# Packing the quarter-wasted product of a two-layer expert kernel into half arrays, a block at a time, with the order of all engines made anew

## The chip, the cores and the metric

The kernel runs on one core of a Trainium2 chip. A core has five engines that run their own instruction streams in order: PE (matrix products; its weight loads, PEld, are separate instructions), DVE and ACT (elementwise work), POOL (here mainly the issuer of indirect DMAs) and SP (the issuer of plain DMAs). The metric is device time in microseconds for one execution; lower is better. Before the change the median of three runs is 1201.41 us (1190.59 to 1201.69).

## What is computed

```python
x  = attention_like_convolution(x, softmax(weight_gen))      # 14336 tokens x 192 channels, 7 taps
lg = x @ w_gate + log1p(exp(x @ w_noise)) * noise            # 8 experts
top2, top2_w = two largest of lg, softmax over the two
for e in range(8):                                           # each expert: 192 -> 1024 -> 192
    out[mask] += top2_w * (relu(x[mask] @ w1[e]) @ w2[e])
```

Inputs and outputs are fp32. The kernel carries each fp32 factor as a pair of fp16 numbers, a high part and a low part, and adds up the products of the parts.

## The kernel before, in words

**Front end.** Tokens come in 14 chunks of 1024. For a chunk, DVE does the convolution (13 multiplications and additions of 128x1536, lines 327 and 337), ACT and DVE split the result into high and low parts (lines 348, 352; tile `rec`, 384 fp16 values a token: 192 high parts, the low parts of channels 128 to 191, the low parts of channels 0 to 127), SP makes transposed copies (line 374), PE computes gate logits (line 381), and DVE picks the two experts and a row in each expert's queue (lines 449 to 558). POOL then scatters the 1024 tokens to the queues in HBM, `xg`, by 16 indirect DMAs (line 411), each behind a tiny memset (line 410). ACT squares the convolution's inputs ahead of it (line 273).

**Rounds and blocks.** Round c takes 256 rows from each of the 8 queues once chunk c is scattered: 8 blocks a round, 14 rounds, and a fifteenth with 128 rows a block. For a block, SP fetches the rows transposed (line 823) into `xT`, three tiles of 128 partitions: x0 the high parts of channels 0 to 127, x1 the high parts of channels 128 to 191 on the lower 64 partitions and their low parts on the upper 64, x2 the low parts of channels 0 to 127. Six `xT` buffers exist.

**First layer.** A block has four steps (two in the last round). A step (`mm1`, line 879) fills one PSUM bank `pm` with two of the eight 128-wide slices of the hidden layer: five products a slice, ten of 128x256 in all. One of the five is W_low x x1 (weight columns 384 to 511). Only the lower 64 of its 128 rows are needed; the upper 64 multiply a low part by a low part, which is negligible. ACT makes `hi` (line 894) and DVE `lo` (line 898) from the bank.

**Second layer.** `mm2` (line 919) takes `hi` and `lo` of a step as stationary operands: 12 products of 192 columns. At a block's end ACT scales the sums (line 931, tile `y`), and POOL adds them to the output by an indirect DMA for each 128 rows (line 936), two a block. In the last round each of these waits for the one before.

**Order.** Nothing is reordered on the chip. A planner (`Sched`) runs at build time: every piece of work is a generator that names its engine, a planned duration and what it waits for, and the planner lays the instructions down in the order in which they would start, ties within `WAIT` going to the higher number in `PR`. The generator `tensor` alternates the steps on PE: `mm1` of a step, then `mm2` of the step two before, so that ACT and DVE have time between. There are five slots, each with a `pm` bank and a `hi` and `lo` tile. The eight experts' weights are split once at the start; for experts in `LOWPE` the low parts are made on PE and ACT (lines 739 to 743), for the others on DVE (lines 710, 717, 719).

Of the kernel before, what the change touches and what calls it, by code (L numbers as in the profile page):

```python
# [8 lines left out]
F16 = mybir.dt.float16  # L9
# [6 lines left out]
P = 128  # L16
NTOK = 14336
NJ = NTOK // P
D = 192
# [22 lines left out]
NEAR = 2  # L42
HURRY = 12
# [6 lines left out]
LOWPE = (0, 4, 5, 6)  # L50
WAIT = 0.29
PR = dict(split=1.0, gate=8.7, conv1=12.1, conv=4.3, route=7.6, idle=8.7, scatter=1.8, stray=2.1, gates=5.7,
          finish=12.3, relu=11.4, norms=4.0, rows=9.0, wload=1.0, due=12.1, undue=4.3)
GL, AL, ML, UL, XL = 3.9, 0.9, 4.4, 17.1, 15.4
# [93 lines left out]
def moe_kernel(ctx, tc, x_lay, wgen, noise, wgn, w1, w2, xg, out):  # L148
# [630 lines left out]
    class Block:  # L779
        pass  # L780
# [16 lines left out]
    def prologues():  # L797

        for c, (k, b) in enumerate(ROUNDS):
# [31 lines left out]
            for e in range(E):  # L831
# [35 lines left out]
    def mm1(si):  # L867

        bi, s = steps[si]
        o = blist[bi]  # L870
        v = slot_of[si]
        pm = (psb if v < PM0 else late[0]).tile([P, 512], F32, name=f"pm{v}")
        for k in range(o.nf):
            f = s * o.nf + k
            w = wres[:, o.e * WE + f * FW:o.e * WE + (f + 1) * FW]
            dst = pm[:, k * o.b:(k + 1) * o.b]
            x0, x1, x2 = (o.xT[:, i, :o.b] for i in range(3))
            for i, (c0, m) in enumerate(((0, x0), (0, x2), (128, x1), (384, x1), (256, x0))):
                nc.tensor.matmul(dst, w[:, c0:c0 + 128], m, start=i == 0, stop=i == 4)  # L879
        hbuf[si] = pm  # L880
# [88 lines left out]
    def tensor():  # L969
# [12 lines left out]
        for si, (bi, s) in enumerate(steps):  # L982
# [10 lines left out]
            slot_of[si], prev_of[si], last[v] = v, last[v], si  # L993
            T["mm1", si] = yield ("PE", 1.09 * o.nf * o.b / 512, lambda: mm1(si), deps)
# [141 lines left out]
```

## Time and profile before

| | |
|---|---|
| median of 3 runs | 1201.41 us (1190.59 to 1201.69) |
| the profiled execution | 1206.64 us, its span 1204.7 us |
| PE busy | 1051.8 us (87%) |
| DVE busy | 825.7 us (69%) |
| POOL busy | 749.8 us (62%) |
| ACT busy | 526.0 us (44%) |
| mean granted PE clock | 0.950 of full speed |

The page sums each engine over the whole span. It also cuts the span into 40 slices of 30 us, with one digit for each (9 is busy 90% or more). A wait is shown behind a row as the idle time before it and what ended it. Since PE is pipelined, the recorded duration of one product is longer than the distance from its start to the next one's start; the distance is what a stream of products costs.

### The profile page before, as it was taken

The numbers are of one execution on the slowest core, as the hardware profiler recorded it, in microseconds if no ns is written. First come the engines' busy times: TensorE is split into PE (matmuls) and PEld (weight loads), VectorE is DVE, ScalarE is ACT, GpSimd is POOL, SyncE is SP. The second block draws the span as 40 slices with busy tenths as digits, with TensorE's granted clock in tenths as the row PEclk, the third lists the DMA queues.
The fourth block names the chain that finished last, engine by engine and source line by source line (L and its number), as shares of the span: only waits on it lengthen the run. The fifth ranks groups of instructions, "written<-read, shape, count | busy, mean of one in ns | idle before, by whom it ended". The sixth has DMA issues, their size and how long they took to land.

```text
span 1204.7 us, 27979 instructions
## 1 busy us (share of the span) xinstructions
PE 1051.8 (87%) x10862; PEld 953.8 (79%) x10862; DVE 825.7 (69%) x1552; ACT 526.0 (44%) x1191; POOL 749.8 (62%) x1013
## 2 busy tenths in 40 slices
PE   1414899797998999999999999989999889999995
PEld 0201499786997999889999889879898779999995
DVE  5898878686795969778887859678885343333331
ACT  6868573342443444443435344434343233333332
POOL 0004368477686868778684858778787867434333
PEclk9755999898998999999999999999999989999998
DMA  9993473665647577485748666365555545434341
GB/s 246 244 283 100 117 170 62 92 145 95 132 88 138 109 125 98 88 161 96 154 78 155 107 117 129 58 131 120 79 91 81 102 74 81 52 54 47 35 41 21
DMA packets 249686, 132.48 MB, mean 110 GB/s; under 512 B 182096, under 2 KB 242000, under 8 KB 247888
## 3 DMA queue, kind: packets, MB, share of 16 engines
q1 hardware_dynamic: 205392, 85.37, 32.3%
q0 software_dynamic: 44160, 45.31, 24.9%
q8 instruction: 85, 1.39, 0.5%
q14 instruction: 49, 0.40, 0.1%
HBM read 38.70 MB, written 58.10 MB: 80 GB/s over the span
## 4 chain that ended last, share of the span: by engine, by line
PE 52%; POOL 15%; DMA 10%; DVE 7%; issue 6%; ACT 6%; SPq 4%; another core or an unknown queue 0%; POOLq 0%; DVEq 0%; ACTq 0%
PE pm L879 27%; PE py L919 24%; POOL xg L411 8%; POOL out L936 7%; DMA xt<-x_lay 3%; DMA out<-y,token 3%; SPq L817 2%; DVE acc L337 2%; DVE tmp L327 2%; DVE lo L898 2%; DMA xg<-rec,pos 1%; DMA xT<-xg 1%; DMA wres<-w 1%; ACT junk L682 1%; ACT junk L273 1%
## 5 line engine op out<-in xcount | busy, mean ns | idle before, releaser
L879 PE MATMUL pm<-xT,wres 128*128 128x256 f16 (+1 forms) x4800 | 594.3, 271 | 30.2 <-DMA xT<-xg 23.4
L936 POOL DMA_INDIRECT out<-y,token x232 | 408.0, 1759 | 254.4 <-ACT y L931 89.3
L898 DVE SCALAR_TENSOR_TENSOR lo<-pm,hi 128x512 f16<-128x512 f32 x464 | 316.1, 686 | 301.1 <-ACT hi L894 261.4
L879 PEld LDWEIGHTS <-wres 128*128 128x128 f16 x4800 | 451.6, 99 | 83.4 <-DMA xT<-xg 21.9
L919 PE MATMUL py<-wres,hi 128*128 128x192 f16 x3712 | 503.3, 247 | 9.8 <-ACT hi L894 4.0
L894 ACT ACTIVATE hi<-pm 128x512 f16<-128x512 f32 x464 | 275.7, 596 | 507.4 <-PE pm L879 407.7
L919 PE MATMUL py<-wres,lo 128*128 128x192 f16 x1856 | 458.6, 247 | 4.5 <-issue 3.0
L919 PEld LDWEIGHTS <-hi 128*128 128x128 f16 x3712 | 341.6, 98 | 23.2 <-issue 8.9
L411 POOL DMA_INDIRECT xg<-rec,pos x224 | 292.0, 1304 | 76.4 <-issue 67.5
L919 PEld LDWEIGHTS <-lo 128*128 128x128 f16 x1856 | 182.3, 98 | 8.5 <-issue 5.5
L337 DVE TENSOR_TENSOR acc<-acc,tmp 128x1536 f32<-128x1536 f32 (+1 forms) x90 | 148.0, 1644 | 1.1
L327 DVE TENSOR_TENSOR tmp<-xt,wt 128x1536 f32<-128x1536 f32 (+1 forms) x90 | 148.2, 1646 | 0.7
L931 ACT ACTIVATE y<-py,gate 128x192 f32<-128x192 f32 x232 | 96.3, 417 | 78.0 <-PE py L919 37.6
L935 POOL MEMSET spacer<- 1x1 f32 x232 | 102.8, 443 | 0.1
L533 POOL TENSOR_SCALAR rec<-rr 128x8 f32<-128x8 f32 x14 | 3.2, 229 | 90.7 <-DVE rr L482 89.8
L410 POOL MEMSET spacer<- 1x1 f32 x224 | 53.3, 238 | 0.1
L273 ACT ACTIVATE junk<-xt 128x192 f16<-128x192 f32 x118 | 42.3, 359 | 23.9 <-DMA xt<-x_lay 22.0
L602 PE MATMUL sums<-ss,ones 128*128 128x2 f32 x32 | 8.1, 333 | 39.4 <-ACT junk L682 39.4
L602 PEld LDWEIGHTS sums<-ss,ones 128*128 128x128 f32 x32 | 7.1, 282 | 43.0 <-ACT junk L682 43.0
L739 PE MATMUL sums<-wres,dg 128*128 128x512 f32 (+1 forms) x48 | 29.3, 698 | 5.3 <-ACT wres L743 3.1
L352 DVE TENSOR_TENSOR rec<-acc,rec 128x512 f16<-128x512 f32 (+2 forms) x30 | 26.8, 900 | 3.1 <-ACT rec L348 2.7
L739 PEld LDWEIGHTS sums<-wres,dg 128*128 128x128 f32 x48 | 9.9, 230 | 22.3 <-ACT wres L743 10.4
(139 smaller groups left out, 514.8 us busy)
## 6 DMA issues: line engine op xcount, KB each, us to landing
xt<-x_lay SPq DMA_DIRECT2D x13, 1344.0 KB
out<-zrec SPq DMA_DIRECT2D x14, 768.0 KB
wres<-w SPq DMA_DIRECT2D x6, 768.0 KB
out<-y,token POOLq DMA_INDIRECT x232
xg<-rec,pos POOLq DMA_INDIRECT x224
wt<-wgen SPq DMA_DIRECT2D x14, 224.0 KB
wres<-w SPq DMA_DIRECT2D x6, 512.0 KB
wres<-w SPq DMA_DIRECT2D x12, 256.0 KB
```

The costliest lines, as they stand in the source:

```text
L273: nc.scalar.activation(q, xtile[s][:, i - first], AF.Square, accum_out=nrm[:, i:i + 1])
L327: V.tensor_mul(tm[key].rearrange("p j (h g) -> p j h g", h=H), xt[:, t:t + n].rearrange("p j (h g) -> p j h g", h=H), w[:, a:a + n].rearra ...
L337: ta = yield ("DVE", cc, lambda: V.tensor_add(tm["acc"], tm["acc"], tm["tmp"]), [])
L410: nc.gpsimd.memset(spacer, 0.0)
L411: i = nc.gpsimd.indirect_dma_start(out=xg, out_offset=bass.IndirectOffsetOnAxis(ap=idx, axis=0), in_=src, in_offset=None)
L879: nc.tensor.matmul(dst, w[:, c0:c0 + 128], m, start=i == 0, stop=i == 4)
L894: nc.scalar.activation(h[0][:, :n], pm[:, :n], AF.Relu)
L898: T["lo", si] = yield ("DVE", dve(n), lambda: nc.vector.scalar_tensor_tensor(h[1][:, :n], pm[:, :n], 0.0, h[0][:, :n], op0=OP.max, op1=OP. ...
L919: nc.tensor.matmul(dst, h[:, cols], w[:, c0:c0 + D], start=begin, stop=f == F // P - 1 and i == 2, skip_group_check=True)
L931: nc.scalar.activation(y[0], o.py[t // 2][:, (t % 2) * D:(t % 2 + 1) * D], AF.Copy, scale=gate_of[o.c][:, o.e, t:t + 1])
L935: nc.gpsimd.memset(spacer, 0.0)
L936: i = nc.gpsimd.indirect_dma_start(out=out, out_offset=bass.IndirectOffsetOnAxis(ap=token[o.c][:, o.e, t:t + 1], axis=0), in_=y[0], in_off ...
```

## The change

From the third round on (`PACK = 2`) the half-empty product is done in half arrays. A second transposed copy (`again`) puts channels 64 to 191 on the 128 partitions of a fourth tile in `xT`, so that the high parts of channels 128 to 191 lie on the upper 64 partitions too. `mm1` then does all steps of a block at once: four full products a slice, eight slices, and behind them eight products with 64 rows each, alternately on the lower and the upper half of the array, into two different PSUM banks. `tensor` lays a block's `mm1` down as one piece and lets one block's steps wait behind it (`BEHIND = 1`). The planner's numbers are other ones, and with them the order of everything; `LOWPE` has experts 4, 5, 7 in place of 0, 4, 5, 6.

```diff
-NEAR = 2
-HURRY = 12
+NEAR = 8
+HURRY = 9
...
+PACK = 2
+BEHIND = 1
+LOWPE = (4, 5, 7)
...
-                o.xT = (blk if v < 3 else late[1]).tile([P, 3, BMAX], F16, name=f"xT{v}", bufs=1)
-                note(nc.sync.dma_start_transpose(o.xT[:, :, :b], xg.bitcast(F16)[bass.ds(base[o.e], b), 0:RD]))
+                o.packed = c >= PACK
+                o.xT = (blk if v < 3 else late[1]).tile([P, 4, BMAX], F16, name=f"xT{v}", bufs=1)
+                note(nc.sync.dma_start_transpose(o.xT[:, 0:3, :b], xg.bitcast(F16)[bass.ds(base[o.e], b), 0:RD]))
+
+            def again(o):
+
+                note(nc.sync.dma_start_transpose(o.xT[:, 3:4, :b], xg.bitcast(F16)[bass.ds(base[o.e], b), 64:D]))
...
+                if c >= PACK:
+                    T["x", bi] = yield ("SP", 1.3, lambda: again(blist[bi]), [], 0.15 * nt)
...
-    def mm1(si):
+    def mm1(si, n):
...
+        for s in range(s0, s0 + n):
+            v = slot_of[si + s - s0]
+            pm = (psb if v < PM0 else late[0]).tile([P, 512], F32, name=f"pm{v}")
+            hbuf[si + s - s0] = pm
+            for k in range(o.nf):
+                f = s * o.nf + k
+                w = wres[:, o.e * WE + f * FW:o.e * WE + (f + 1) * FW]
+                dst = pm[:, k * o.b:(k + 1) * o.b]
+                parts.append((w, dst, k))
+                ops = [(0, x0), (0, x2), (128, x1), (256, x0)] + ([] if o.packed else [(384, x1)])
...
+        if o.packed:
+            m = len(parts) // 2
+            for a, b in zip(parts[:m], parts[m:]):
+                for (w, dst, k), h, x in ((a, slice(0, 64), x1), (b, slice(64, P), o.xT[:, 3, :o.b])):
+                    nc.tensor.matmul(dst, w[h, 384:512], x[h], start=False, stop=k == o.nf - 1, skip_group_check=True)
...
-            v = min(range(SLOTS if late else PM0), key=lambda i: last[i])
-            deps = [("x", bi), ("low1", o.e)] + ([("lo", last[v])] if last[v] >= 0 else [])
+            m = o.n if o.packed_(late) else 1
+            vs = sorted(range(SLOTS if late else PM0), key=lambda i: last[i])[:m]
+            deps = [("x", bi), ("low1", o.e)] + [("lo", last[v]) for v in vs if last[v] >= 0]
...
-                if len(pend) > DEPTH - 1 or r is None or r > sch.free["PE"] + 0.4:
+                if len(pend) > (DEPTH - 1 if m == 1 else o.n - 1 + BEHIND) or r is None or r > sch.free["PE"] + 0.4:
...
+            us = 1.09 * o.nf * o.b / 512 * m
+            if m > 1:
+                us = us * 0.9 + 0.2
+            t = yield ("PE", us, lambda: mm1(si, m), deps)
```

On PE in the middle of the run, before: the last product of a step's first layer (`pm`) and the second layer (`py`) of an earlier step (`hi1`, `lo1`). Numbers in names tell buffers and tiles apart.

```order
L879 MATMUL pm0_9249<-xT3_8731,wres_94 128x256
L919 LDWEIGHTS hi1_9203
L919 MATMUL py_9189<-wres_94,hi1_9203 128x192
L919 LDWEIGHTS hi1_9203
L919 MATMUL py_9189<-wres_94,hi1_9203 128x192
L919 LDWEIGHTS lo1_9204
L919 MATMUL py_9189<-wres_94,lo1_9204 128x192
```

On PE of the change, the end of a block's `mm1` (its 32 full products into `pm1`, `pm2`, `pm3`, `pm4` stand ahead of these rows): the half products, and the first of the second layer.

```order
L901 MATMUL pm3_10102<-xT1_9484,wres_94 128x256
L901 LDWEIGHTS wres_94
L901 MATMUL pm2_10093<-xT1_9484,wres_94 128x256
L901 LDWEIGHTS wres_94
L901 MATMUL pm4_10111<-xT1_9484,wres_94 128x256
L901 LDWEIGHTS wres_94
L901 MATMUL pm2_10093<-xT1_9484,wres_94 128x256
L901 LDWEIGHTS wres_94
L901 MATMUL pm4_10111<-xT1_9484,wres_94 128x256
L940 LDWEIGHTS hi2_10024
L940 MATMUL py_10145<-wres_94,hi2_10024 128x192
```

Where ten full products and twelve of the second layer took turns, a block now has 32 full and 8 half products in a row, then 48 of the second layer; the halves alternate between two banks.

On POOL at the start, before: the scatter of chunk 1 (`xg<-rec_576`) and the first blocks' additions to the output.

```order
L411 DMA xg<-rec_576,pos 131072x196
L935 MEMSET spacer 1x1
L936 DMA out<-y_1206,token 14592x192
L935 MEMSET spacer 1x1
L936 DMA out<-y_1263,token 14592x192
L410 MEMSET spacer 1x1
```

On POOL of the change, from the end of chunk 0's scatter (`rec_287`) on: chunk 1's (`rec_502`).

```order
L413 DMA xg<-rec_287,pos 131072x196
L535 TENSOR_SCALAR rec_502<-rr 128x8
L537 COPY rec_502<-tokc 128x8
L412 MEMSET spacer 1x1
L413 DMA xg<-rec_502,pos 131072x196
```

Chunk 1's last scatter stands behind 4 additions to the output in place of 10.

On DVE, before, in the middle of chunk 0's routing: two weight subtractions (`wres`) stand between the count `th` and the row numbers.

```order
L490 TENSOR_TENSOR ln_631<-o0_609,o1_610 128x8x8
L496 TENSOR_REDUCE th_636<-ln_631 128x8
L710 SCALAR_TENSOR_TENSOR wres_94<-wres_94,q_377 128x8x192
L510 TENSOR_TENSOR gg_642<-mm_607 128x8
L717 SCALAR_TENSOR_TENSOR wres_94<-wres_94,q_377 128x8x128
L515 SCALAR_TENSOR_TENSOR uu_654<-keep_109,ln_631 128x64
```

On DVE of the change, the same place:

```order
L492 TENSOR_TENSOR ln_546<-o0_527,o1_528 128x8x8
L498 TENSOR_REDUCE th_548<-ln_546 128x8
L354 TENSOR_TENSOR rec1_502<-acc_405,rec1_502 128x8x64
L512 TENSOR_TENSOR gg_554<-mm_525 128x8
L517 SCALAR_TENSOR_TENSOR uu_561<-keep_109,ln_546 128x64
```

The subtractions have gone from here (one of 128x8x192 stands some 20 instructions ahead), and part of chunk 1's split has come in.

## Rows read from the trace of the kernel before

**Rows 1.** The page: busy time by engine, and PE in 40 slices of 30 us.
```profile
PE 1051.8 (87%) x10862; PEld 953.8 (79%) x10862; DVE 825.7 (69%) x1552; ACT 526.0 (44%) x1191; POOL 749.8 (62%) x1013
...
PE   1414899797998999999999999989999889999995
```

**Rows 2.** Busy time by stretch: rounds 2, 3, 4, 5, 6 to 11, 12, the last.
```profile
core 0: us, PE busy (x) PEld busy (x) DVE busy (x) ACT busy (x) POOL busy (x), PEclk, DMA share, GB/s
...
298.90:373.90 75.00, 69.62 (x733) 64.77 (x734) 58.51 (x115) 31.12 (x73) 53.36 (x68) 0.96 0.53 106
373.90:442.50 68.60, 67.90 (x707) 62.59 (x708) 54.51 (x98) 29.67 (x69) 53.15 (x67) 0.97 0.61 117
442.50:512.90 70.40, 68.42 (x734) 63.39 (x733) 57.69 (x117) 30.12 (x72) 54.05 (x70) 1.00 0.69 114
512.90:582.90 70.00, 68.48 (x731) 63.44 (x732) 57.09 (x112) 29.19 (x70) 51.81 (x74) 1.00 0.70 138
582.90:1021.80 438.90, 417.45 (x4383) 384.23 (x4381) 306.70 (x598) 172.82 (x390) 333.77 (x445) 0.98 0.57 101
1021.80:1088.40 66.60, 66.60 (x707) 62.98 (x705) 23.58 (x41) 25.41 (x49) 29.84 (x41) 1.00 0.39 53
...
1155.00:1204.70 49.70, 35.83 (x538) 35.60 (x536) 12.25 (x21) 13.65 (x26) 16.11 (x21) 0.89 0.30 29
```

**Rows 3.** Timeline of PE, one step's two layers: start us, us, engine line.
```profile
621.99 1.25 PE L879 MATMUL pm<-xT,wres 128*128 128x256 f16 x10
623.08 0.33 PE L919 MATMUL py<-wres,hi 128*128 128x192 f16 x2
...
624.07 1.25 PE L879 MATMUL pm<-xT,wres 128*128 128x256 f16 x10
```

**Rows 4.** Groups of instructions by shape: busy us, mean ns of one, idle before.
```profile
L879 PE MATMUL pm<-xT,wres 128*128 128x256 f16 x4480 | 573.8, 275 | 30.2 <-DMA xT<-xg 23.4 <-issue 6.2
...
L879 PEld LDWEIGHTS <-wres 128*128 128x128 f16 x4800 | 451.6, 99 | 83.4 <-DMA xT<-xg 21.9 <-issue 17.0
...
L898 DVE SCALAR_TENSOR_TENSOR lo<-pm,hi 128x512 f16<-128x512 f32 x464 | 316.1, 686 | 301.1 <-ACT hi L894 261.4 <-issue 33.6 <-ACT junk L273 3.7
...
L894 ACT ACTIVATE hi<-pm 128x512 f16<-128x512 f32 x464 | 275.7, 596 | 507.4 <-PE pm L879 407.7 <-remote 38.6 <-issue 20.9
...
L327 DVE TENSOR_TENSOR tmp<-xt,wt 128x1536 f32<-128x1536 f32 x78 | 136.7, 1752 | 0.3
```

**Rows 5.** Timeline of PE where rounds 1 to 4 begin; the wait in brackets.
```profile
217.59 0.82 PE L879 MATMUL pm<-xT,wres 128*128 128x256 f16 x3 [6.23 <-DMA xT<-xg]
...
298.90 1.46 PE L879 MATMUL pm<-xT,wres 128*128 128x256 f16 x6 [8.82 <-DMA xT<-xg]
...
373.87 1.46 PE L879 MATMUL pm<-xT,wres 128*128 128x256 f16 x6 [5.38 <-DMA xT<-xg]
...
442.46 1.25 PE L879 MATMUL pm<-xT,wres 128*128 128x256 f16 x10
```

**Rows 6.** Timeline of POOL, first and last scatter of chunk 4.
```profile
383.04 1.00 POOL L411 DMA_INDIRECT xg<-rec,pos  x1 [0.26 <-DVE lim L557]
...
430.62 0.96 POOL L411 DMA_INDIRECT xg<-rec,pos  x1 [0.23 <-issue]
```

**Rows 7.** Timeline of DVE and POOL at the end of chunk 0's routing.
```profile
94.84 1.82 DVE L710 SCALAR_TENSOR_TENSOR wres<-wres,q 128x1536 f16<-128x1536 f32 x1
...
96.66 1.28 DVE L717 SCALAR_TENSOR_TENSOR wres<-wres,q 128x1024 f16<-128x1024 f32 x1
...
104.28 1.19 POOL L411 DMA_INDIRECT xg<-rec,pos  x1 [11.17 <-issue]
```

**Rows 8.** The fetch's line: instructions, duration ns (least, median, most).
```profile
L823 SPq DMA_TRANSPOSE xT<-xg x120: 1179/1215/5638, 136.7 to 1162.6; - x120
```

**Rows 9.** The chain that ended last, near the end.
```profile
1188.35 3.51 DMA out<-y,token
...
1192.61 3.58 DMA out<-y,token
```

More of the change, by code (lines that the diff above doesn't have):

```diff
@@ L49 @@
 DEPTH = 3
[L50 to L54, printed above, removed]
+PACK = 2
+BEHIND = 1
+LOWPE = (4, 5, 7)
+WAIT = 0.34
+PR = dict(split=11.1, gate=9.8, conv1=12.5, conv=3.6, route=11.4, idle=5.8, scatter=9.0, stray=3.0,
+          gates=10.0, finish=11.6, relu=11.4, norms=1.5, rows=4.2, wload=2.1, due=10.1, undue=11.9)
+GL, AL, ML, UL, XL = 1.4, 0.3, 1.5, 13.5, 9.8
 class Sched:
@@ L779, in moe_kernel, with packed_ @@
     class Block:
-        pass
+        def packed_(self, late):
+            return self.c >= PACK
     steps, blist = [], []
@@ L865, in moe_kernel @@
     hbuf = {}
-    def mm1(si):
-        bi, s = steps[si]
+    def mm1(si, n):
+        bi, s0 = steps[si]
         o = blist[bi]
[L871 to L880, printed above, removed]
+        x0, x1, x2 = (o.xT[:, i, :o.b] for i in range(3))
+        parts = []
+        for s in range(s0, s0 + n):
[8 more added lines that the diff above has]
+                ops = [(0, x0), (0, x2), (128, x1), (256, x0)] + ([] if o.packed else [(384, x1)])
+                for i, (c0, m) in enumerate(ops):
+                    nc.tensor.matmul(dst, w[:, c0:c0 + 128], m, start=k == i == 0, stop=not o.packed and i == 4
+                                     and k == o.nf - 1, skip_group_check=True)
+        if o.packed:
[3 more added lines that the diff above has]
+                    nc.tensor.matmul(dst, w[h, 384:512], x[h], start=False, stop=k == o.nf - 1, skip_group_check=True)
     def relus(si):
@@ L980, in second @@
                 sch.spawn(finish(bj, t), PR["finish"])
-        for si, (bi, s) in enumerate(steps):
+        si = 0
+        while si < len(steps):
+            bi, s = steps[si]
             o = blist[bi]
             at[0] = bi
-            v = min(range(SLOTS if late else PM0), key=lambda i: last[i])
-            deps = [("x", bi), ("low1", o.e)] + ([("lo", last[v])] if last[v] >= 0 else [])
+            m = o.n if o.packed_(late) else 1
+            vs = sorted(range(SLOTS if late else PM0), key=lambda i: last[i])[:m]
+            deps = [("x", bi), ("low1", o.e)] + [("lo", last[v]) for v in vs if last[v] >= 0]
             while pend:
                 r = sch.ready(deps)
-                if len(pend) > DEPTH - 1 or r is None or r > sch.free["PE"] + 0.4:
+                if len(pend) > (DEPTH - 1 if m == 1 else o.n - 1 + BEHIND) or r is None or r > sch.free["PE"] + 0.4:
                     yield from second()
@@ L992, in tensor @@
                     break
-            slot_of[si], prev_of[si], last[v] = v, last[v], si
-            T["mm1", si] = yield ("PE", 1.09 * o.nf * o.b / 512, lambda: mm1(si), deps)
-            if s == o.n - 1:
-                T["used", bi] = T["mm1", si]
-            pend.append(si)
-            sch.spawn(relus(si), PR["relu"])
+            for i, v in enumerate(vs):
+                slot_of[si + i], prev_of[si + i], last[v] = v, last[v], si + i
+            us = 1.09 * o.nf * o.b / 512 * m
+            if m > 1:
+                us = us * 0.9 + 0.2
+            t = yield ("PE", us, lambda: mm1(si, m), deps)
+            for i in range(m):
+                T["mm1", si + i] = t
+                pend.append(si + i)
+                sch.spawn(relus(si + i), PR["relu"])
+            si += m
+            if s + m == o.n:
+                T["used", bi] = t
         while pend:
```

## The prediction

> **What bounds the kernel now.** Start with the page. PE is busy 87% of the span, DVE 69%, and in the 40 slices PE has an 8 or 9 in nearly every one from the sixth on [rows 1]. So PE's work is the bound of the long middle, and work taken from PE there should shorten it. Then the busy time by stretch: rounds 12 and onward are PE and nothing else (66.60 of 66.60 us), while rounds 2 to 5 take 75.0, 68.6, 70.4 and 70.0 us, with PE busy 67.9 to 69.6 of them, clock stretches included [rows 2]. Third, the places where a round begins: rounds 1, 2 and 3 begin after waits of 6.23, 8.82 and 5.38 us for `xT`, the fetched rows; round 4 begins without one [rows 5]. So the early rounds are held by the chain from a chunk's routing over its scatter on POOL to the fetch, the later ones by PE. A gain on PE counts whole only in the later ones.
>
> A block costs 66.60 / 8 = 8.32 us on PE [rows 2]. Ten products of the first layer take 623.08 - 621.99 = 1.09 us, so one slot of 256 columns is 0.109 us; twelve of the second take 624.07 - 623.08 = 0.99 us [rows 3]. Four steps of 2.08 make the block.
>
> **PE's work.** The change turns 8 of a block's 40 first-layer products into half-array ones. If the two halves run side by side, 8 slots become 4: 4 x 0.109 = 0.436 us saved a block. The number of instructions and weight loads stays the same. The trace has no half-array product and no change between whole and half, so this is bounded from both sides. From below: a change of kind costs nothing. From above: the product in flight must end first, and the next weights can't be loaded behind it. One product is recorded with 275 ns and its slot is 109, so 166 ns are overlap that is lost, and a weight load is 99 ns [rows 4]; 0.265 us a change, two changes a block, 0.53 us. Half the bound is my choice, 0.26 us, because each row of the loads shows overlap with products, and it is likely that a part of it survives. Net 0.18 us a block: 8.14 us. The bounds are 7.88 and 8.41.
>
> The Trainium skill bears on this choice. Its page TensorEngine Tiling (Array Packing), section Key Properties, states that changing the tiling mode drains TensorE; by that rule the upper bound, 8.41 us, holds and the block becomes dearer than 8.32. Its page TensorE: Matmul & The Clock Gate, section Measured speedup vs the span model, gives one product's time and about 4 ns for each further tile as the span of row tiles; as an estimate by that page the saving is 4 x 0.105 = 0.42 us. No row here shows either.
>
> **The order of a block.** Steps no longer take turns; a block's whole first layer (about 3.9 us) runs, then second-layer work. Of the 96 packed blocks of 256 rows, in the order as printed, 30 have two steps of the block before and then at least one of their own; most others have three or four old ones first. After the first layer ends, the first `hi` takes 0.60, `lo` 0.69 [rows 4], and I allow 0.25 for two hand-overs: 1.54 us. Two old steps cover 1.98 us, so 0.44 us are to spare in those 30 and 1.4 us with three old steps. The banks for the next block's first layer are asked for 3.9 us after the end and the last of them that matters is free at 1.54 + 2 x 0.69 = 2.9. So I cost this at nothing; the cover is gone if DVE is inside a convolution instruction (1.75 us [rows 4]) when `hi` arrives, and that is a rival below.
>
> **The second copy.** 104 more transposing DMAs on SP, of 1.215 us each by their kind's median [rows 8]: 9.7 us a round on a queue that issues the 8 others of the round for the same price. The first half product that needs the copy stands behind 33 others of its block, 3.6 us, so the copy of a first block hides there. Queued behind it on SP are the next block's fetch and the loads of the front end; each comes 1.2 us later, against 8 us a block. Nothing is charged; without cover, 1.2 us at each of the round starts that wait.
>
> **The start.** On DVE two weight subtractions of 1.82 and 1.28 us leave chunk 0's routing, but another stands a little ahead of it and 1.9 us of chunk 1's split come in. Three experts' low parts are made on PE in place of four, so DVE gets 1.82 + 1.28 + 1.28 = 4.4 us more of them; they stand behind chunk 0's routing, while POOL scatters, and DVE has time there. Chunk 0's scatter (104.28 us) waits for the last of the routing [rows 7]. Bounds 0 and 7 us earlier; I take 4. Chunk 1's routing now ends ahead of every `lo` (behind 6 before), and its scatter has 4 additions to the output in its way in place of 10, so the 6.23 us wait at round 1 goes [rows 5]. But round 2's rows depend on chunk 2, whose routing stands behind 38 `lo` (39 before) and whose scatter starts behind 18 additions, as before. It now stands 81.3 us from round 1's start to round 2's, 298.90 - 217.59, and a part of round 1's gain only waits there. Round 2 begins 8 us earlier: 4 from the head, 4 from routing that has less ahead of it.
>
> **Rounds 2 to 5.** The chain for round 4 as it is: round 3 begins at 373.87, chunk 4's first scatter comes 9.2 us later, its last 47.6 us after that (383.04 to 430.62 [rows 6]), and 11.8 us later round 4 begins (442.46 [rows 5]): 68.6 us. After: its routing stands behind 99 `lo` in place of 100, that is behind the first block's whole first layer and three `lo`, some 7 us and the last routing instructions, about 9 as now. Between first and last scatter stand 10 additions (8 before) for chunk 4, 8 (10 before) for chunks 3 and 5. So this chain gives 67 to 69 us a round where PE needs 8 x 8.14 + 1.6 = 66.7 (the 1.6 is what PE is busy beyond 66.6 in such rounds, 67.9 to 68.5 [rows 2]). I take 67.5 three times and 66.5 once: 269 for 284.0, 15 us less. Bounds: 0 if the chain keeps its time, 18 if it gives way to PE.
>
> **Rounds 6 to 13.** From 582.9 to 1155.0 [rows 2], 64 blocks at 0.18 us: 11.5 us less. I leave the waits in there as they are.
>
> **The end.** The last round's 49.7 us [rows 2] end in a chain of eight additions, one every 1192.61 - 1188.35 = 4.26 us [rows 9], which no product shortens. Its first one comes later by a block's first layer, 2.2 us at 128 rows, and the half block more that is waiting: 3 us longer.
>
> **Sum.** -8 - 15 - 11.5 + 3 = -31.5 us. The profiled execution took 1206.64 us for a span of 1204.7, 5.2 above the median of 1201.41, so 1175 in its terms and 1170 in the median's. My own range for this case is 1152 to 1188.
>
> **Rivals.**
> *The change of kind costs nothing.* Block 7.88: 64 x 0.436 = 28 in rounds 6 to 13, the early rounds still held by the scatter chain. -8 - 15 - 28 + 3 = -48: 1153. For it: PE overlaps everything else it does, loads included [rows 4].
> *The whole drain is paid.* Block 8.41. Rounds 2 to 5 at 8 x 8.41 + 1.6 = 68.9, 8 us less in all; rounds 6 to 13 are 6 longer. -8 - 8 + 6 + 3 = -7: 1194. For it: 166 ns of each product are overlap that a change can cost. The Trainium skill's rule on changing the tiling mode (TensorEngine Tiling (Array Packing), Key Properties) is this rival.
> *The front end keeps its pace.* POOL is busy 52 to 54 us and DVE 54 to 58 of each early round's 70 [rows 2], in fixed order and with waits between; at 66 us they must be busy 80 to 88%. If rounds 2 to 11 keep their old time, what remains is the head, 16 blocks x 0.18 and the end: -8 - 3 + 3 = -8: 1193. Against it: neither is full.
> *Late low parts (slower).* Where `lo` of a block's first step is one convolution instruction late, PE stands 1.75 - 0.44 = 1.3 us in the 30 blocks with two old steps and 0.35 in some 20 with three, ahead of the last convolution: 46 us. 1216, slower by over 1%; from 31.5 us lost it is no gain at all, from 43.5 a loss over 1%. For it: DVE waits for `hi` 261 us in all [rows 4], so its order already stalls on PE. Against it: the planner places `lo` high.
> *The halves run one after another.* Nothing saved and 0.53 us paid: 8.85 a block, +34 in rounds 6 to 13, +4 in 2 to 5. 1201 - 8 + 34 + 4 + 3 = 1234.
>
> **Chances.** Forecast 0.43, no cost of the change 0.15, whole drain 0.14, front end 0.12, late low parts 0.10, halves in turn 0.06. Faster by over 1% (below 1189, about what a measurement can tell): the first two and half of the whole drain, 0.65. Slower by over 1% (above 1213): 0.06 and most of the late low parts, 0.13. Within 1%: 0.22. The range 1138 to 1212 leaves out the last rival, half of the late low parts and the lower edge of the cheapest case.
>
> **What would show it.** The half products' starts: pairs 0.11 us apart if side by side, 0.22 if in turn; the first product behind a change of kind shows its price. Round 1 without a wait for `xT`, round 2 at about 290 us. Rounds 12 and 13 at 65.1 us each. Waits of PE for `lo` or `hi` in the middle would make me wrong, as would waits for `xT` at rounds 6 and later.

## The result, and the profile after

The median is 1178.12 us (1177.55 to 1178.96) against 1198.24 us for the kernel before in the same session (1190.59 to 1201.69): a ratio of 0.984, 95% interval 0.980 to 0.987. The forecast was 1170 us in a range of 1138 to 1212; in medians the change gained 20.1 us, where 31.5 were forecast. A second measurement beside the experiments gave 0.983 (0.979 to 0.988). The profiled execution took 1178.96 us for a span of 1177.1.

The page of the changed kernel, busy time by engine and PE in 40 slices, answers to [rows 1]:

```profile
PE 1009.3 (86%) x10838; PEld 897.8 (76%) x10838; DVE 831.0 (71%) x1555; ACT 515.6 (44%) x1181; POOL 737.4 (63%) x1013
...
PE   0012899998999999899999989899699999999992
```

PE does 42.5 us less work than before, and the span is only 27.6 us shorter. The busy time by stretch tells where (rounds 2, 3, 4, 5, 6 to 11, 12, and the last; columns as in [rows 2], to which these rows answer):

```profile
285.70:359.10 73.40, 68.18 (x719) 60.38 (x720) 59.31 (x114) 29.40 (x71) 52.67 (x71) 0.94 0.72 129
359.10:424.60 65.50, 65.50 (x721) 58.73 (x719) 56.37 (x102) 29.29 (x71) 51.36 (x66) 0.98 0.62 120
424.60:495.60 71.00, 64.81 (x721) 58.20 (x719) 53.65 (x99) 30.34 (x71) 51.90 (x68) 0.99 0.65 119
495.60:564.70 69.10, 69.10 (x743) 61.52 (x744) 57.43 (x109) 29.70 (x70) 50.88 (x73) 0.96 0.76 135
564.70:988.00 423.30, 400.75 (x4383) 359.34 (x4382) 321.74 (x621) 171.05 (x392) 317.29 (x435) 0.98 0.68 117
988.00:1052.80 64.80, 64.80 (x707) 58.52 (x705) 21.84 (x39) 24.10 (x48) 35.13 (x52) 1.00 0.51 71
...
1118.60:1177.10 58.50, 35.78 (x539) 33.89 (x536) 11.17 (x20) 13.10 (x27) 18.00 (x23) 0.82 0.23 26
```

Round 2 begins at 285.7 (298.9 before), rounds 2 to 5 take 279.0 us (284.0), rounds 6 to 13, from 564.7 to 1118.6, 553.9 us (572.1), the last 58.5 us (49.7). -13.2 - 5.0 - 18.2 + 8.8 = -27.6 us, the difference of the spans. That is 7.5 us more than the medians differ by, because the profiled execution of the kernel before was a long one (1206.64 us, the median 1198.24); the four parts hold that difference too.

**The half products.** A block in round 12 on the timeline of PE (start us, us, what). It answers to [rows 3].

```profile
1044.69 3.66 PE L895 MATMUL pm<-xT,wres 128*128 128x256 f16 x32
1048.28 0.61 PE L901 MATMUL pm<-xT,wres 64*128 64x256 f16 x8
1048.82 0.34 PE L940 MATMUL py<-wres,hi 128*128 128x192 f16 x2
...
1052.79 3.66 PE L895 MATMUL pm<-xT,wres 128*128 128x256 f16 x32
```

From the first half product to the start of the second layer it is 1048.82 - 1048.28 = 0.54 us, not 8 x 0.109 = 0.87 (the 0.61 us of the row include the recorded end of the last one, which overlaps what follows). In the trace's single records the two of a pair start 3 or 4 ns apart, and the pairs 109 to 120 ns. The first half product starts 205 ns behind the full one before it, the first of the second layer 202 ns behind the last half, where 109 is the usual slot. A block now takes 1052.79 - 1044.69 = 8.10 us.

**Waits.** Groups by shape answer to [rows 4], and the round starts on PE to [rows 5]:

```profile
L895 PE MATMUL pm<-xT,wres 128*128 128x256 f16 x3712 | 438.9, 275 | 11.2 <-DMA xT<-xg 9.0 <-DVE lo L919 2.2
...
L940 PE MATMUL py<-wres,lo 128*128 128x192 f16 x1856 | 459.4, 248 | 18.1 <-DVE lo L919 18.0
```
```profile
213.74 0.93 PE L895 MATMUL pm<-xT,wres 128*128 128x256 f16 x7
...
285.71 1.66 PE L895 MATMUL pm<-xT,wres 128*128 128x256 f16 x8 [3.51 <-DMA xT<-xg]
...
355.60 0.34 PE L940 MATMUL py<-wres,lo 128*128 128x192 f16 x1 [5.21 <-DVE lo L919]
...
495.56 1.67 PE L895 MATMUL pm<-xT,wres 128*128 128x256 f16 x7 [5.52 <-DMA xT<-xg]
```

PE's waits for `xT` fell from 23.4 us [rows 4] to 9.0, and round 1 has none. In their place PE waits 18.0 us for `lo`. The longest of these waits ends at 843 us, in round 9 (timelines of DVE and PE, DVE's list of waits, and one stretch):

```profile
828.45 0.27 DVE L531 TENSOR_TENSOR dd<-o,uu 128x64 f32<-128x64 f32 x1
839.84 0.18 DVE L861 TENSOR_TENSOR gate<-meta,eid 128x16 f32<-128x16 f32 x1 [11.12 <-DMA meta<-xg]
```
```profile
DVE gate L861 <- DMA meta<-xg: 53.1, 10, 11.1
```
```profile
843.44 0.34 PE L940 MATMUL py<-wres,lo 128*128 128x192 f16 x1 [9.89 <-DVE lo L919]
...
846.93 4.77 PE L895 MATMUL pm<-xT,wres 128*128 128x256 f16 x32
```
```profile
832.00:846.00 14.00, 4.11 (x36) 3.74 (x34) 5.73 (x15) 1.96 (x5) 8.48 (x16) 0.63 0.65 87
```

A DVE instruction of 0.18 us, the gate of a round, waits 11.1 us for its `meta`, the token numbers and gate terms of the rows, which SP fetches once the chunk is scattered. `lo` and the routing of the next chunk stand behind it; PE stands 9.9 us. DVE waits this way 53.1 us in all. And the wait costs more than itself: the granted clock is 0.63 in that stretch, and the 32 full products after it are recorded as 4.77 us, not 3.66.

What held this `meta` up was the scatter, and no fetch on SP: SP waited 21.3 us for the scatter to land, and its fetch began 2.7 us after the chunk's last scatter (timelines of POOL and SP, and SP's list of waits from 815 to 842 us):

```profile
831.07 0.98 POOL L413 DMA_INDIRECT xg<-rec,pos  x1 [0.23 <-issue]
```
```profile
833.78 4.40 SPq L820 DMA_DIRECT2D meta<-xg  x8
```
```profile
SPq L820 <- DMA xg<-rec,pos: 21.3, 2, 20.1
```

### The profile page after: what moved, and what is told of

It is laid out like the page before. It is cut to its first block, busy times and chain, and to the rows that moved or that the text cites. A ratio compares the mean times of both kernels' runs of the same rounds, so it can differ in the third digit from the quotient of the medians.

```text
span 1177.1 us, 28220 instructions
## 1 busy us (share of the span) xinstructions
PE 1009.3 (86%) x10838; PEld 897.8 (76%) x10838; DVE 831.0 (71%) x1555; ACT 515.6 (44%) x1181; POOL 737.4 (63%) x1013
## 4 chain that ended last, share of the span: by engine, by line
PE 66%; POOL 9%; DMA 8%; DVE 6%; ACT 4%; issue 4%; SPq 2%; DVEq 0%; POOLq 0%; ACTq 0%
PE py L940 31%; PE pm L895 29%; POOL out L957 4%; POOL xg L413 4%; PE pm L901 4%; DMA wres<-w 2%; SPq L820 2%; DMA xt<-x_lay 2%; DVE tmp L329 2%; DVE acc L339 2%; PE sums L741 1%; DMA out<-y,token 1%; DMA xg<-rec,pos 1%; DMA meta<-xg 1%; ACT junk L275 1%
## 5 line engine op out<-in xcount | busy, mean ns | idle before, releaser
L940 PE MATMUL py<-wres,hi 128*128 128x192 f16 x3712 | 480.6, 248 | 3.4 <-ACT y L952 3.4
L895 PE MATMUL pm<-xT,wres 128*128 128x256 f16 (+1 forms) x3968 | 454.5, 272 | 11.2 <-DMA xT<-xg 9.0
L915 ACT ACTIVATE hi<-pm 128x512 f16<-128x512 f32 x464 | 263.3, 596 | 451.2 <-PE pm L901 352.4
L919 DVE SCALAR_TENSOR_TENSOR lo<-pm,hi 128x512 f16<-128x512 f32 x464 | 304.2, 685 | 205.9 <-ACT hi L915 196.3
L895 PEld LDWEIGHTS <-wres 128*128 128x128 f16 x3968 | 379.3, 99 | 55.9 <-DMA xT<-xg 9.5
L940 PEld LDWEIGHTS <-hi 128*128 128x128 f16 x3712 | 330.4, 98 | 24.4 <-issue 20.8
L413 POOL DMA_INDIRECT xg<-rec,pos x224 | 266.4, 1189 | 74.2 <-issue 55.2
L940 PEld LDWEIGHTS <-lo 128*128 128x128 f16 x1856 | 182.6, 98 | 20.3 <-DVE lo L919 20.1
L952 ACT ACTIVATE y<-py,gate 128x192 f32<-128x192 f32 x232 | 91.5, 418 | 63.1 <-PE py L940 56.9
L901 PE MATMUL pm<-xT,wres 64*128 64x256 f16 (+1 forms) x832 | 61.8, 268 | 0.0
L901 PEld LDWEIGHTS <-wres 64*128 64x128 f16 x832 | 31.5, 94 | 23.3 <-issue 20.2
L861 DVE TENSOR_TENSOR gate<-meta,eid 128x16 f32<-128x16 f32 (+1 forms) x15 | 2.7, 178 | 53.6 <-DMA meta<-xg 53.1
```

The lines of the kernel that those rows point to most:

```text
L413: i = nc.gpsimd.indirect_dma_start(out=xg, out_offset=bass.IndirectOffsetOnAxis(ap=idx, axis=0), in_=src, in_offset=None)
L895: nc.tensor.matmul(dst, w[:, c0:c0 + 128], m, start=k == i == 0, stop=not o.packed and i == 4 and k == o.nf - 1, skip_group_check=True)
L901: nc.tensor.matmul(dst, w[h, 384:512], x[h], start=False, stop=k == o.nf - 1, skip_group_check=True)
L915: nc.scalar.activation(h[0][:, :n], pm[:, :n], AF.Relu)
L919: T["lo", si] = yield ("DVE", dve(n), lambda: nc.vector.scalar_tensor_tensor(h[1][:, :n], pm[:, :n], 0.0, h[0][:, :n], op0=OP.max, op1=OP. ...
L940: nc.tensor.matmul(dst, h[:, cols], w[:, c0:c0 + D], start=begin, stop=f == F // P - 1 and i == 2, skip_group_check=True)
```

## The experiments

They ran on several chips, on which the kernel before took 1212 to 1218 us; each is held against it on its own chip, as a ratio. Where an expectation is in microseconds, read it against the 1198 of the first session.

**1. Whole products in the new order.** 

```diff
-                for (w, dst, k), h, x in ((a, slice(0, 64), x1), (b, slice(64, P), o.xT[:, 3, :o.b])):
-                    nc.tensor.matmul(dst, w[h, 384:512], x[h], start=False, stop=k == o.nf - 1, skip_group_check=True)
+                for w, dst, k in (a, b):
+                    nc.tensor.matmul(dst, w[:, 384:512], x1, start=False, stop=k == o.nf - 1, skip_group_check=True)
```

> The changed kernel with its order, its second copy and its whole-block first layer kept; only the eight half-array products of a block become eight full-array ones again, one after another. Theory (the gain of the middle comes from the halves): in rounds that PE bounds, each block loses the 0.436 us of four slots and gets back the 0.19 us of two changes of kind, +0.245 us a block. Rounds 12 and 13 go from 64.8 and 64.7 us to 66.7 each; six such rounds give +12, rounds 2 to 5 and 9, 10, which wait for other things, +0 to +5: 1188 to 1196 us in all. Rival (the new order of all engines made the gain, the halves add nothing): 1175 to 1181 us, rounds 12 and 13 below 65.5.

Ratio 0.987 (0.982 to 0.993). Stretch of round 12, this kernel:

```profile
1007.70:1074.30 66.60, 66.60 (x706) 62.98 (x705) 22.20 (x39) 24.83 (x50) 35.62 (x54) 1.00 0.54 71
```

Round 12 is as the theory has it, 66.6 us, exactly as before the change. The total is not: against 0.984 with halves, it is 0.4 points (4 to 5 us) more, where the theory wanted 10 to 18 us and the rival at most 3, and the two intervals overlap. So the halves do save on PE, but little of it reaches the end.

**2. All halves on one half of the array.** The loop over the pair is replaced again.

```diff
+                for w, dst, k in (a, b):
+                    nc.tensor.matmul(dst, w[0:64, 384:512], x1[0:64], start=False, stop=k == o.nf - 1, skip_group_check=True)
```

> The changed kernel, but all eight half products of a block lie on the lower half of the array (with the lower 64 weights and rows), so no two can run side by side; the upper half's operand, and with it the use of the second copy, is left out. Theory (side by side is what saves; a half product alone takes a full slot, and the change of kind costs 0.096 us each, whatever half it is): eight starts 0.109 us apart, block 8.09 + 0.436 = 8.53 us, rounds 12 and 13 at 68.2 us each, in all 1198 to 1212 us, slower than the run with whole products by 0.19 us a block. Rival 1 (a half product is cheaper by itself, since only half the rows are filled): starts well below 0.109 us apart, rounds 12 and 13 under 66.5. Rival 2 (the 0.096 us comes from alternating halves, not from the change between whole and half): no gap at either end, block as with whole products, rounds at 66.7.

Ratio 0.997 (0.994 to 1.000). Stretch of round 12, and the half products of a block on PE's timeline:

```profile
1006.60:1074.90 68.30, 68.30 (x707) 61.48 (x705) 22.59 (x40) 24.82 (x50) 35.26 (x52) 1.00 0.51 70
```
```profile
1040.73 3.66 PE L895 MATMUL pm<-xT,wres 128*128 128x256 f16 x32
1044.32 1.04 PE L901 MATMUL pm<-xT,wres 64*128 64x256 f16 x8
1045.29 0.34 PE L940 MATMUL py<-wres,hi 128*128 128x192 f16 x2
```

From the first half product to the start of the second layer it is 0.97 us in place of 0.54: a half product alone takes a whole slot, and all of the saving is in the pairs. Both rivals fall: the starts are 109 to 120 ns apart, and the first half product again comes 205 ns behind the full one, so alternation isn't what costs it. The total lies a little below the theory's 1198 to 1212 us, which as a ratio are 1.000 to 1.012.

**3. Twice the changes of kind.** The loop over the pairs stands in `halves`, and a block of 256 rows calls it twice.

```diff
+            if o.packed and (len(parts) == 8 or o.n == 4 and len(parts) == 4):
+                halves(o, parts)
+                parts = []
```

> The changed kernel, but in the blocks of 256 rows the half products come in two groups of four, each behind four slices of full products: four changes of kind a block in place of two, with the same products. Theory (a change of kind costs 0.096 us on PE, 0.19 a pair): rounds 12 and 13 at 64.75 + 8 x 0.19 = 66.3 us each; in all 1184 to 1192. Rival (the longer distance at the ends of the halves is the hand-over from the first layer to the second, which stays one a block): one further distance of 0.1 us at most, rounds 12 and 13 at 65.0 to 65.5, in all 1176 to 1182.

Ratio 0.989 (0.987 to 0.992). Stretch of round 12:

```profile
1010.50:1077.00 66.50, 66.50 (x707) 57.22 (x705) 22.19 (x39) 24.81 (x50) 35.47 (x54) 1.00 0.53 70
```

66.5 - 64.8 = 1.7 us a round, 0.21 a block for two more changes: 0.1 us each. By the starts a block takes 8.31 us here and 8.10 in the changed kernel. The rival's 65.0 to 65.5 is ruled out.

**4. The order alone**: experiment 1, and the second copy is not fetched either.

```diff
-                    T["x", bi] = yield ("SP", 1.3, lambda: again(blist[bi]), [], 0.15 * nt)
+                    T["x", bi] = yield ("SP", 1.3, lambda: None, [], 0.15 * nt)
```

> The order of the changed kernel with whole products (as in the run with whole products before) and without the second copy, which those do not use: what the new order alone is worth. Theory (the copy is hidden on SP, the order gives the earlier rounds 1 and 2, the halves the rest): the same as the run with whole products within 3 us, 0.985 to 0.990 of before, rounds 12 and 13 at 66.6 us. Rival (the 104 further transposing fetches, 1.2 us each on SP, delay the fetches of the round starts that PE waits for): faster than with the copy by 5 to 15 us, with shorter waits of PE for `xT` at the starts of rounds 2 to 6.

Ratio 0.977 (0.972 to 0.982). With neither half products nor copies the kernel is at least as fast as with both. The theory fell: against experiment 1, which differs by the copies alone and ran on another chip, it is 1.0 point (12 us) less, though the two intervals just touch. The rival has this size right, but not its place: PE's waits for `xT` are 2.5 us in all here and 4.2 in experiment 1.

**5. Halves without the copy**: the changed kernel with the line of experiment 4, its upper halves reading `x1`.

> The changed kernel in its order with its half products side by side, but the second copy is not fetched; the upper halves read the low parts that lie there in the first copy, so this part of the sum (high parts of channels 128 to 191 with the low weights, every second one) is left out. It is the fourth corner beside: order alone (whole products, no copy) 0.977 of before, order and copy (whole) 0.987, order, copy and halves 0.983. Theory (the copies cost 8 to 12 us, by the fetches and `meta` that come later, and the halves are worth 5 to 9): 0.969 to 0.974 of before, rounds 12 and 13 at 64.7 us. Rival (the copies cost nothing, the difference is noise of the measurement): like the changed kernel, 0.980 to 0.986. Rival 2 (without the copies the scatter chain bounds, and halves are worth nothing): like the order alone, 0.975 to 0.979.

Ratio 0.977 (0.973 to 0.981): the number of rival 2; that the scatter chain is the reason is not shown. The four corners are, each with the time that rounds 2 to 11 took in its trace,

| | no second copy | second copy |
|---|---|---|
| whole products | 0.977, 704.2 us | 0.987, 714.5 us |
| half products | 0.977, 708.8 us | 0.984 (0.984 and 0.983), 702.3 and 707.3 us |

Over both rows, the copies cost 0.8 points, some 10 us, with an uncertainty of 0.5 worked out from the four intervals. Over both columns, the halves gain 0.2 points, with the same uncertainty: nothing that can be told from zero. The corners come from several chips, and the traces, one execution each, don't settle either price: they show the copies' price only with whole products, and the halves as a loss without copies and a gain with them. The new order gains 2.3 points. What in it does (a block's first layer as one piece, the planner's numbers, `LOWPE`) was not tested. Rounds 2 to 11 as a stretch, order alone and then halves without copy:

```profile
290.90:995.10 704.20, 683.89 (x7277) 637.38 (x7278) 549.12 (x1041) 288.22 (x673) 528.81 (x708) 0.99 0.61 112
```
```profile
292.10:1000.90 708.80, 669.43 (x7277) 593.38 (x7278) 549.26 (x1041) 287.14 (x673) 524.21 (x708) 0.98 0.63 111
```

PE does 14.5 us less work with the halves, and its idle time grows from 20.3 to 39.4 us. What was saved there turned into waiting. Only rounds 12 and 13 keep the gain (131.3 us in all, 134.2 with the order alone).

**6. Gates later**, and **7. gates later with the order alone**. 

```diff
-            sch.spawn(gates(c, tm), PR["gates"])
+            sch.spawn(gates(c, tm + (8.0 if c > 1 else 0.0)), PR["gates"])
```

> The changed kernel, with the two small DVE instructions that read `meta` (gate and token of a round) planned 8 us later from round 2 on, so that they stand behind more work of DVE; the planner lays the rest down anew around them. Theory (they stand ahead of their data, DVE stands still on them 53 us in all, and `lo` and the routing queue behind): DVE's wait for `meta` under 10 us, PE's waits for `lo` (20 us in all in the profile) under 6, rounds 9 and 10 at 66 to 71 us in place of 77 to 79; 8 to 20 us less than the changed kernel. Rival (the gates are then late for `y` and the additions on POOL, or DVE merely waits for `hi` instead): within 4 us of the changed kernel.

> Order alone (whole products, no second copy), and the gates planned 8 us later. Theory (the gates stand still only because the copies make `meta` late: without copies DVE waits for it 11.9 us in all, against 33.7 with them): at most 4 us better than order alone, 0.974 to 0.978 of before. Rival (the later gates are worth their 9 us whatever delays `meta`): 0.967 to 0.971, as good as or better than the changed kernel with later gates (0.974).

Ratios 0.974 (0.969 to 0.978) and 0.972 (0.968 to 0.976). DVE's list of waits in run 6:

```profile
DVE gate L861 <- DMA meta<-xg: 7.8, 4, 2.7
```

In the changed kernel on the same chip that row read 33.7 us, in its first profile 53.1. The gain on the changed kernel is about 1 point (9 us at the medians, 1191.55 to 1182.49). Rounds 8 and 9, which the expectation calls 9 and 10, take 65.0 and 67.8 us; they took 77.4 and 77.0 in the changed kernel on this chip. But round 7 now takes 81.7 us in place of 70.6, and rounds 2 to 11 as a whole hardly change. The changed kernel's rounds 2 to 11 on this chip, then those of run 6 and its round 7:

```profile
291.50:998.80 707.30, 670.56 (x7276) 593.07 (x7277) 546.64 (x1041) 286.81 (x673) 517.69 (x707) 0.99 0.68 119
```
```profile
290.00:996.50 706.50, 674.42 (x7277) 595.01 (x7278) 549.80 (x1040) 285.67 (x673) 534.69 (x711) 0.98 0.68 120
640.30:722.00 81.70, 72.09 (x743) 63.75 (x744) 58.88 (x105) 31.31 (x72) 58.84 (x81) 0.92 0.74 134
```

So the edit is a gain by the medians, but it is not shown that the gates' wait was what cost the 9 us: the planner laid the whole order down anew, and in these two traces a stall moved from two rounds into another. Without copies the same edit gives 0.5 points, within the uncertainty; 0.972 lies between that expectation's theory and its rival. Experiment 7 has the lowest ratio of all, with 6 and 9 close beside it: that is the change with neither its half products nor its copies. All three beat both kernels.

**8. Last round not packed**, and **9. with gates later**. 

```diff
-                o.packed = c >= PACK
+                o.packed = PACK <= c < NC
```

(and so in the two other places that ask for `PACK`).

> The changed kernel, but the last round (128 rows a block) works as before: steps in turn, whole products, no second copy. Theory (the end got longer because a block's first layer is laid down as a piece and a further block waits behind it, so the first of the eight serial additions comes 17.4 us after the round's start in place of 12.0): first addition 12 to 13 us after the start, the round at 52 to 55 us in place of 59.5, in all 1171 to 1174. Rival (the end is long for what stands behind the last addition, 11.2 us in place of 7.8, or for the place of other instructions): less than 2 us gained, 1175 or more.

> Both edits: the gates 8 us later and the last round as before the change. Theory: the two gains add up, 12 to 26 us less than the changed kernel, last round 53 to 56 us. Rival (the early rounds' chain of scatters takes back what DVE gains): within 6 us of it.

Ratios 0.980 (0.973 to 0.987) and 0.974 (0.970 to 0.978). The first can't tell theory from rival; the second is the same as experiment 6, so the two gains do not add up as the theory had it. The last round, plain and packed, both with later gates:

```profile
1127.10:1183.20 56.10, 35.84 (x538) 35.61 (x536) 11.74 (x20) 13.95 (x27) 17.98 (x23) 0.84 0.22 27
```
```profile
1127.10:1185.10 58.00, 35.80 (x539) 33.91 (x536) 11.17 (x20) 13.10 (x27) 18.03 (x23) 0.84 0.22 27
```

1.9 us of the 8.8: the packing of the last round is not the main cause of the longer end. The first serial addition still comes 15.2 us after the round's start (1142.34 - 1127.1; 16.3 packed), where the theory had 12 to 13. Between runs 6 and 9 the total is the same, as the rival has it; of its two reasons, what stands behind the last addition is 3.4 us (see the end below), and the place of other instructions was not tested alone.

**10. Copy within the chip.** ACT fills the upper 64 partitions from the lower, gates later.

```diff
-                note(nc.sync.dma_start_transpose(o.xT[:, 3:4, :b], xg.bitcast(F16)[bass.ds(base[o.e], b), 64:D]))
+                nc.scalar.activation(o.xT[64:128, 3, :o.b], o.xT[0:64, 1, :o.b], AF.Copy)
...
```

The planner's entry for it goes from SP to ACT, and the gates are as in experiment 6.

> The changed kernel, but the upper 64 partitions of the fourth tile are filled by a copy of ACT within the chip (64 x 256, one a block) in place of the second transposing fetch, and the gates are 8 us later; the planner lays the rest down anew. An estimate for one copy by the 596 ns of a 128x512 `hi`: 0.3 to 0.4 us, 3 us a round on an engine that is busy 44%. Theory (the halves gain in full once SP and the DMA queues are free of 104 fetches): 0.966 to 0.972 of before, PE without waits for `lo` over 6 us in all. Rival (ACT's copies wait in its order for the fetched rows, `hi` queues behind them): ACT idle 10 us or more ahead of the copies, PE waiting for `hi` or `lo`, 0.975 or more.

Ratio 0.976 (0.973 to 0.980). ACT's list of waits:

```profile
ACT xT L832 <- DMA xT<-xg: 47.7, 29, 5.8
```

The rival has the total, and its mechanism, ACT standing ahead of its copies, is there; PE's waits for `lo` are 4.8 us all the same, as the theory wanted. The fetches taken from SP brought nothing that experiment 6 had not.

**11. DVE relieved.** `short` is one product of 128x192 in place of 128x1536.

```diff
+                if c >= 4:
+                    tn = yield ("DVE", cc, short, [])
+                    ta = yield ("DVE", cc, short, [])
+                    continue
                 tn = yield ("DVE", cc, lambda: mul(t), [])
```

> The changed kernel in its order, with DVE relieved: from chunk 4 on, twelve of the convolution's thirteen 128x1536 instructions (six products, six additions, 1.75 us each) handle one eighth of their columns and their result is not used, so that the convolution there has one tap in place of seven (this part is left out; the experts that tokens go to are others, as many a round). DVE has some 17 us less work in each of rounds 3 to 11. Theory (rounds 2 to 11 take 70 to 71 us whatever PE is spared, since the front end, DVE's work above all, keeps its pace; what the half products save turns into small waits of PE): freed from it, these rounds go to what PE needs, 8 x 8.09 + 1.6 = 66.3 us, and rounds 4 to 11 lie below the 68.2 that whole products would need; 20 to 35 us less than the changed kernel, 0.953 to 0.967 of before. Rival (DVE is not what holds the rounds: POOL's row of scatters and additions, each of which waits for a block's result, closes the circle by itself): rounds 3 to 11 still at 69 to 71 us on the mean, less than 10 us gained, 0.976 or more.

Ratio 0.987 (0.983 to 0.992): not faster, rather slower. Rounds 2 to 11, and lists of waits of DVE and POOL:

```profile
288.70:1010.70 722.00, 680.64 (x7280) 598.10 (x7278) 398.75 (x1041) 287.00 (x673) 457.57 (x705) 0.98 0.67 116
```
```profile
DVE lo L927 <- ACT hi L923: 349.2, 173, 10.8
```
```profile
POOL out L965 <- ACT y L960: 252.8, 90, 8.4
```

DVE has 150 us less to do in these rounds, and they take 72 us each on the mean. So the theory that DVE's work bounds them falls. The work taken away turned into DVE waiting for `hi` (349 us in the whole run, 201 in the second profile of the changed kernel) and POOL waiting for `y` (253 us, 120 there). The rival has the outcome; its reason, POOL's row, was not tested. What bounds these rounds is open. A candidate that no run tested: `hi` waits for the second layer of an older step, since a block takes four of the five slots at once. ACT's list of waits before, and in experiment 4:

```profile
ACT hi L894 <- PE py L919: 7.3, 4, 2.9
```
```profile
ACT hi L915 <- PE py L940: 68.9, 109, 5.6
```

This would tie PE, ACT and DVE in a loop of short waits: PE's waits ahead of products of the second layer sum to 13.2 us in rounds 2 to 11 before, 17.6 with the order alone, 21.2 and 24.5 in the two traces of the changed kernel, 26.5 with halves and no copy and 26.1 in the last run. But the row doesn't follow the times: it reads 41.0 us in the first trace of the changed kernel, 138.9 in experiment 3 and 81.7 in the last run. More slots would test it.

## Why the prediction was right, and where it was not

The time was right (1170 forecast, 1178 measured), and so was the sign. The reason was not: 26.5 of the 31.5 us were to come from cheaper blocks on PE and the early rounds that follow them, and the runs give the packing itself nothing that can be measured. The order that came with it made the gain (0.977 of before by itself), and the prediction had it gain at the start and in the rounds that follow it, and nothing from round 6 on. That the total fits is luck: its four terms miss by 5.2, 10, 6.7 and 5.8 us, two of them each way, and cancel to 3.9.

**A block on PE: right.** 8.14 us forecast, 8.10 measured. Half of the bound was a good choice for the change of kind: 0.26 us a block forecast, 0.19 by the starts (205 + 202 - 2 x 109 ns) and 0.21 by experiment 3. The rivals without a cost (7.88), with the whole drain (8.41) and with halves in turn (8.85; experiment 2 shows what that would be, 8.54) are out. A change costs 0.1 us, well under half of the 0.265 us that the rival took for it. The Trainium skill's rule that a change of the tiling mode drains TensorE (TensorEngine Tiling (Array Packing), Key Properties) fits a gap at each change; it gives no price.

**The start: 13.2 us in place of 8, from other parts.** Chunk 0's scatter came 6.3 us earlier, within the 0 to 7 (104.28 us in [rows 7]; 101.58 in the second profile of the changed kernel, on another chip); of the 4 us at the head 0.4 arrived. POOL, then PE:

```profile
97.97 1.97 POOL L413 DMA_INDIRECT xg<-rec,pos  x1 [6.31 <-ACT junk L684]
```
```profile
139.84 0.33 PE L742 MATMUL sums<-wres,minus 128*128 128x384 f16 x1
140.00 1.25 PE L895 MATMUL pm<-xT,wres 128*128 128x256 f16 x10
```

PE's first block waits behind the low parts of the weights on PE itself, laid down ahead of it; it starts at 140.0, where before it started at 140.4 after a wait for `xT`. The prediction followed the rows to the fetch and not PE's own queue. The gain came in rounds 0 and 1 (3.5 and 9.3 us shorter), the 6.23 us wait among it.

**Rounds 2 to 5: 5 us in place of 15.** The chain's estimate (67 to 69 us a round) holds for rounds 3 and 5 (65.5, 69.1) and not for 2 and 4 (73.4, 71.0): in round 2 lies the wait of 5.2 us for `lo`, and round 4 ends in one of 5.5 for `xT`.

**Rounds 6 to 13: 18.2 us in place of 11.5, from another source.** "I leave the waits in there as they are" is the step that failed; [rows 2] show PE idle for 438.90 - 417.45 = 21.5 us of rounds 6 to 11. Of the 18.2 us only rounds 12 and 13, 1.8 and 0.8 us by their stretches, are clean PE time (at the end of round 13 one more second-layer step stands ahead of the next round). Order alone, on its own chip, took 557.3 us for the same rounds. In the middle the order removed a stall (round 11 took 79.0 us, 68.0 with the order alone, now 64.5), and the changed kernel has a new one (round 9, with the wait for `meta`, takes 78.8 us; before 69.6, with the order alone 69.2). Round 8 is as long as it was (77.3 us, before 76.5).

**The second copy: not free by the ratios, and why is open.** "Nothing is charged" failed by the ratios: 0.3 to 1.3 points, some 10 us. It is not that the copies make `meta` late on SP. In the traces of all four corners the first `meta` of rounds 2 to 13 starts 2.5 to 3.8 us after the chunk's last scatter, with copies and without, and SP had issued what stands ahead of it at least 6.9 us before that scatter's end. DVE's waits for `meta` don't follow the copies either: 53.1, 33.7 and 32.9 us in the corners with them, 11.9 and 23.9 without, but 13.2 in experiment 2, which fetches them too, and 14.8 before. How a copy would delay anything was not measured alone.

**The order of a block: not nothing.** The cover (two old steps, 1.98 us) was counted against ACT's and DVE's time, but not against the slots; the row of `hi` waiting for `py` above was left out, though no run shows what it costs. The rival of late low parts had the right place (PE waiting for `lo`, 18 us) and a different cause: a tiny instruction that waits for a DMA, not a long one. The rival of the front end that keeps its pace was near the outcome, that PE's saving is lost in rounds 2 to 11, though the new order did shorten them (722.9 us before, 704.2 with the order alone, 702.3 now); and the relieved DVE shows that it isn't DVE's load that sets the pace.

**The end: 8.8 us in place of 3.** The eight serial additions take what they took (31.0 us from first to last, 30.0 before, 4.26 us apart in [rows 9]). The first came 1134.92 - 1118.6 = 16.3 us after the round's start, 1166.96 - 1155.0 = 12.0 before, and behind the last stand 11.2 us in place of 7.8. The first addition and the count on DVE before, then POOL, ACT and DVE now:

```profile
1166.96 1.55 POOL L936 DMA_INDIRECT out<-y,token  x1 [3.41 <-DMA out<-y,token]
```
```profile
1192.47 0.17 DVE L1038 TENSOR_TENSOR cnt<-run,con 128x8 f32<-128x8 f32 x1 [3.25 <-DMA out<-y,token]
```

```profile
1134.92 1.55 POOL L957 DMA_INDIRECT out<-y,token  x1 [2.81 <-DVE lo L919]
...
1165.87 1.55 POOL L957 DMA_INDIRECT out<-y,token  x1 [2.69 <-DMA out<-y,token]
```
```profile
1120.92 0.60 ACT L915 ACTIVATE hi<-pm 128x512 f16<-128x512 f32 x1 [3.67 <-PE pm L901]
1121.42 0.42 ACT L952 ACTIVATE y<-py,gate 128x192 f32<-128x192 f32 x1
```
```profile
1170.09 0.17 DVE L1069 TENSOR_TENSOR cnt<-run,con 128x8 f32<-128x8 f32 x1 [17.82 <-DMA out<-y,token]
```

A `y` of an old block stands on ACT behind a `hi` that needs the new block's whole first layer, so its addition is late: the last four additions of round 13 now stand 4.1 to 4.6 us apart, where before those of a block came 1.85 us apart. And the final count on DVE now waits for the last addition, where before it was done earlier (1192.47, the last addition came at 1196.94). What stands behind the last addition is longer by 3.4 us. Neither was in the sum.

## What to carry to other kernels

Work taken from the busiest engine is worth its time only in stretches in which nothing else waits; take the price of a slot from such a stretch (here rounds 12 and 13), and expect elsewhere that it turns into waits. When a change brings a new order with it, measure the order without the change: here it was, as far as the runs can tell, the whole gain. A short instruction that waits for a DMA on an in-order engine holds up what stands behind it (PE stood 9.9 us here), so look at where it stands before looking at what it does. Then sum the whole stretch again: here one stall went and another came.

## What the runs showed of the hardware

- Two half-array products side by side start 3 or 4 ns apart and share one slot (0.54 us from the first of eight to the next instruction, against 0.97 on one half). The Trainium skill's few nanoseconds for each further tile (TensorE: Matmul & The Clock Gate, Measured speedup vs the span model) agree.
- A change between full and half products costs 0.1 us at either end (205 and 202 ns from start to start, 109 without a change), the same with all halves on the lower half as with both in turn. That is the size of one weight load (94 to 99 ns in the groups by shape); that it is one is not shown.
- A 9.9 us wait of PE was followed by some 3.5 us of second-layer products at 160 ns a start in place of 82, at the lower of the two clock levels (granted clock 0.50 from 840 to 845 us), and the next block's first layer came slower too (4.77 us in place of 3.66). By the granted clock in stretches of 5 us, PE spent some 37 us at that level between its first block and the last round in the first profile of the changed kernel, 17 with the order alone.
